# A delta-rule recurrence followed by a SoLU block: the 64x64 products of a slot in three runs, ScalarE in program order, two copies moved to it

## The chip, the core and the metric

The kernel runs on one core of a Trainium2 chip. Its engines work side by side from queues of their own: TensorE (PE; its weight loads are listed apart as PEld), VectorE (DVE), ScalarE (ACT), GpSimd (POOL) and SyncE (SP), which only issues transfers. TensorE writes to PSUM, VectorE and ScalarE read it[...]. The metric is the device time of one execution in microseconds, the median of several runs. A profiled execution gives the trace; its span runs from the first to the last instruction.

## What is computed

Two stages. The first is a recurrence over 768 time steps for 4 batches of 8 heads, with a state of 40x40 per head:

```python
y[:, :, t] = np.einsum('bhd,bhde->bhe', rt, state)
Sa = np.einsum('bhde,bhe->bhd', state, at)
state_decay = state * wt[:, :, None, :] - np.einsum('bhd,bhe->bhde', Sa, bt)
state = state_decay + np.einsum('bhd,bhe->bhde', vt, kt)
```

The result, brought to 3072 tokens of 320 numbers, goes into the second stage:

```python
h = x @ w_in                                   # 320 -> 1024
e = np.exp(h - h_max); sm = e / (np.sum(e) + 1e-09)
solu = h * sm
ln = (solu - mu) / np.sqrt(var + 1e-06) * g_ln
out = ln @ w_out                               # 1024 -> 320
```

`w_in` and `w_out` arrive as 64-bit floats, and the kernel narrows them to 32 bits itself.

## The kernel before, in words

Time is cut into chunks of 64 steps. One index i stands for one chunk of two batches (the two batches fill the 128 partitions, 64 each), so there are 24 of them; even and odd i belong to the two pairs of batches and carry separate states. Within a chunk the recurrence is written as products of 64x64 or smaller matrices, one for each of 2 batches x 8 heads, placed four at a time in the quarters of TensorE's array. A set of 16 such products is 32 instructions in the trace. The 64x64 triangular system of each head is solved through inverses of its two 32x32 diagonal blocks, computed on VectorE by elimination (`invert`, 30 steps of two operations each for two chunks at a time, L415 and L417). The blocks travel through DRAM so that they lie one per partition: `norm` stores its masked product `nt` (L388), `spread` loads the blocks (L399), `invert` stores the inverses (L422), `bring` loads them (L434, L436).

A main loop runs over slots i = -1 to 27. A slot holds work for several chunks at different stages. j = i + 5 is prepared: `decay` (logarithm of w, cumulated by a product into `pcum`, two exponentials), `decay_turned` (transposes `pei`), `scaled` (k and b times the inverse decay, on GpSimd), `front` (transposes `pa` and `pb` of a and b), `norm` (`pnt`). For i+1, `attend_kv` and `attend_rs` transpose k, v, r and the state (`pk`, `pv`, `pr`, `pst`), `scores` makes `ps`, `couple` makes `py`, `close` makes `pz`. For i, `carried` and `driven` make the right side `px` from the state and the values, `solved` applies the inverse (`pu`), `answered` makes `pl`, `read` makes the output and the new state `pyo`, `leave` takes both off PSUM. Between these stands the second stage for earlier chunks: `hidden` (products `h`, six parts of three k tiles by two halves), `exped` (maximum, exponential), `weighed` and `spreadof` (product, statistics), `folded` (transposes `plnT`), `output` (products `po`, eight of 320 columns).

In six places of a slot of the kernel before, small products stand between wide ones: `carried` and `driven`; `solved`; `norm`; `answered`; `scores` and `couple`; `close` and `read`. The part k=2 of `hidden` uses half of the array's rows. Where two groups of small products add into the same PSUM numbers from different rows of the array, `fence` (L257) drains TensorE between them: in `driven` and in the second half of `read`.

The order: TensorE, GpSimd, VectorE and SP run in the order in which the Python code calls them; only ScalarE's instructions are ordered by a scheduler. `some(n)` emits the next n elimination steps, and the tables `shares` (steps in each of four places of a slot) and `narrowed` (weights to narrow in each of two places) distribute VectorE's work. Narrowing (`split`) takes two operations on VectorE, three on ScalarE and three on VectorE for each weight tile; there are 13 of them, two before the loop and 11 in slots -1 to 3. [...]two buffers of two banks (`banks`: pu, ps, py, pnt, pl, pz, pyo, px in turn), one buffer of two banks for `h`, two buffers of one bank (`bank`: all transposes, `pcum`, `po`, `pmean`).

## Time and profile before

| | |
|---|---|
| median of 3 runs | 639.37 us (638.72 to 640.19) |
| the profiled execution | 639.79 us, its span 637.7 us |
| mean granted TensorE clock | 0.930 |
| busy: PE, DVE, POOL, ACT | 567.5, 461.9, 269.1, 245.3 us |
| weight loads (PEld) | 399.6 us |
| HBM traffic | 84 GB/s over the span |

The page of the profile gives busy time by engine, then 40 slices of the span, then queues, the chain of work that ended last, and the costliest groups. Line numbers (L254) are those of the kernel; L254 is the helper through which all small products and `h` go, so they are told apart by the tile that they write. Ends of TensorE's instructions are modelled; starts are better evidence.

### The profile page before, as it was taken

The page shows a single profiled execution, that of the slowest core. Times are in us where ns is not written, and L with a number is a line of the kernel's source. Part 1 is how long each engine was busy: PE and PEld are TensorE (multiplying, and loading weights), DVE is VectorE, ACT ScalarE, POOL GpSimd, SP SyncE. Part 2 cuts the span into 40 slices and gives each one's busy share as a digit, 9 for nine tenths or more (in the row PEclk, how much of TensorE's full clock was granted, in tenths as well). Part 3 has the DMA queues.
Part 4 walks back from the last instruction along what each step waited for, and adds up shares of the span by engine and source line. Part 5 has one row for each costly group of instructions (what it writes and reads, how often), then busy time and mean ns, then how long its engine had stood idle before and what let it go on. Part 6 is the DMA issues. An engine that isn't in the chain of part 4 may idle for free.

```text
span 637.7 us, 26729 instructions
## 1 busy us (share of the span) xinstructions
PE 567.5 (89%) x11451; PEld 399.6 (63%) x11451; DVE 461.9 (72%) x1286; ACT 245.3 (38%) x498; POOL 269.1 (42%) x444
## 2 busy tenths in 40 slices
PE   5245677988999999999999999999999999999995
PEld 3134555756577677667667767666776666766653
DVE  4678799999878778778878777787887796443431
ACT  3412545554334434433443443344243333332221
POOL 3334345574274444445543642743544642222200
PEclk9665676688999999999999999999999999999998
DMA  8939896474355535544554553654423422210000
GB/s 166 159 73 169 170 164 131 107 152 87 71 110 93 111 87 95 107 93 103 103 120 79 108 116 73 119 107 95 91 53 70 98 49 49 51 36 26 24 20 21
DMA packets 217868, 59.92 MB, mean 94 GB/s; under 512 B 203216, under 2 KB 213048, under 8 KB 217752
## 3 DMA queue, kind: packets, MB, share of 16 engines
q1 hardware_dynamic: 200984, 34.47, 31.7%
q0 software_dynamic: 11376, 19.25, 12.6%
q10 hardware_dynamic: 5392, 4.51, 2.5%
q8 instruction: 90, 1.47, 1.0%
q14 instruction: 26, 0.21, 0.1%
HBM read 40.10 MB, written 13.37 MB: 84 GB/s over the span
## 4 chain that ended last, share of the span: by engine, by line
PE 71%; DVE 13%; DMA 6%; issue 4%; ACT 2%; SPq 2%; POOL 1%; DVEq 0%; ACTq 0%; POOLq 0%
PE h L254 16%; PE po L703 14%; PE pyo L254 7%; PE px L254 4%; PE pu L254 3%; DVE uu L417 3%; PE plnT L692 3%; PE ps L254 3%; DVE prod L415 3%; PE pl L254 2%; PE pr L334 2%; PE pnt L254 2%; PE pk L334 2%; PE pa L334 2%; PE pz L254 2%
## 5 line engine op out<-in xcount | busy, mean ns | idle before, releaser
L254 PE MATMUL h<-w_in,xT 128*128 128x512 f32 (+1 forms) x288 | 121.6, 614 | 0.0
L415 DVE TENSOR_TENSOR prod<-blk,uu 128x30 f32<-128x30 f32 (+4 forms) x360 | 99.0, 275 | 24.0 <-DMA blk<-nt_dram 14.0
L703 PE MATMUL po<-w,lnT 128*128 128x320 f32 x384 | 113.5, 440 | 0.0
L417 DVE TENSOR_TENSOR uu<-uu,prod 128x30 f32<-128x30 f32 (+4 forms) x360 | 101.9, 283 | 12.4
L703 PEld LDWEIGHTS po<-w,lnT 128*128 128x128 f32 x384 | 70.5, 190 | 29.3 <-issue 2.3
L655 DVE TENSOR_REDUCE nmax<-h 128x1 f32<-128x1024 f32 x24 | 29.4, 1224 | 60.0 <-PE h L254 59.9
L388 POOL DMA_DIRECT2D nt_dram<-nt x20 | 18.3, 916 | 119.0 <-DVE nt L362 97.7
L254 PEld LDWEIGHTS h<-w_in,xT 128*128 128x128 f32 (+1 forms) x288 | 38.9, 190 | 21.9 <-issue 20.8
L623 POOL TENSOR_TENSOR st<-tot,ex 104x160 f32<-104x160 f32 x44 | 22.1, 520 | 70.4 <-DVE tot L619 68.2
L681 POOL TENSOR_TENSOR rs<-c,mhalf 128x1 f32<-128x1 f32 x24 | 13.4, 559 | 91.0 <-DVE c L680 89.6
L635 POOL DMA_DIRECT2D xT<-x x96 | 48.7, 512 | 0.0
L254 PE MATMUL pyo<-lv,kb 64*64 64x104 f32 x768 | 38.6, 274 | 6.0 <-DVE lv L362 3.3
L693 ACT COPY lnT<-plnT 128x512 f32<-128x512 f32 x48 | 26.1, 589 | 43.3 <-PE plnT L692 43.3
L399 POOL DMA_DIRECT2D blk<-nt_dram x42 | 33.3, 800 | 13.0 <-DMA nt_dram<-nt 12.7
L658 ACT ACTIVATE e<-h,nmax 128x1024 f32<-128x1024 f32 x24 | 26.8, 1115 | 28.6 <-DVE nmax L655 27.5
L254 PE MATMUL pyo<-lu,kb 64*64 64x104 f32 x768 | 37.2, 266 | 0.0
L664 DVE TENSOR_TENSOR e<-h,e 128x1024 f32<-128x1024 f32 x24 | 29.4, 1225 | 10.1 <-ACT e L658 10.1
L276 POOL DMA_DIRECT2D raw_r<-in_r_dram x48 | 34.9, 729 | 0.3 <-issue 0.3
L672 DVE BATCH_NORM_STATS2 bs<-e 128x6 f32<-128x512 f32 x48 | 30.9, 686 | 0.8
L707 ACT ACTIVATE osb<-po,rs 128x320 f32<-128x320 f32 x24 | 12.7, 528 | 48.5 <-PE po L703 29.6
L254 PEld LDWEIGHTS pnt<-aT,bT 40*64 40x64 f32 x768 | 14.6, 144 | 26.5 <-issue 25.0
L254 PEld LDWEIGHTS pyo<-lv,kb 64*64 64x64 f32 x768 | 23.9, 145 | 11.3 <-issue 7.7
(130 smaller groups left out, 1127.0 us busy)
## 6 DMA issues: line engine op xcount, KB each, us to landing
blk<-nt_dram POOLq DMA_DIRECT2D x42, 128.0 KB, 4.2
nt_dram<-nt POOLq DMA_DIRECT2D x20, 256.0 KB, 3.5
raw_w<-in_w_dram SPq DMA_DIRECT2D x48, 80.0 KB
a<-in_a_dram SPq DMA_DIRECT2D x48, 80.0 KB
raw_r<-in_r_dram POOLq DMA_DIRECT2D x48, 80.0 KB, 3.3
lv<-in_v_dram SPq DMA_DIRECT2D x48, 80.0 KB
out_dram<-osb ACTq DMA_DIRECT2D x24, 160.0 KB
raw_b<-in_b_dram SPq DMA_DIRECT2D x44, 80.0 KB
```

Of the source, the lines that this page charges most:

```text
L254: nc.tensor.matmul(o, lhsT=lhsT, rhs=rhs, start=start, stop=stop, skip_group_check=True)
L276: queue.dma_start(out=x[half(p), :, 0:D], in_=ap[2 * bp + p, :, ci * C:(ci + 1) * C, :].rearrange("h t d -> t h d"))
L334: nc.tensor.transpose(out=t[0:W2, j * P:(j + 1) * P], in_=x[:, 2 * j:2 * j + 2].rearrange("p a b -> p (a b)")[:, 0:W2], identity=ident)
L399: queue.dma_start(out=nb[home:home + Q], in_=blocks[n][:, Q * e:Q * e + Q, Q * e:Q * e + Q])
L415: nc.vector.tensor_tensor(out=t, in0=nb[:, j:j + 1, j + 1:Q].to_broadcast([P, n_c, m]), in1=u[:, 0:n_c, j:j + 1].to_broadcast([P, n_c, m]) ...
L417: nc.vector.tensor_tensor(out=u[:, 0:n_c, j + 1:Q], in0=u[:, 0:n_c, j + 1:Q], in1=t, op=ALU.subtract)
L635: nc.gpsimd.dma_start(out=xT[to:to + Q, 2], in_=x[at + P - 3 * D:at + D, 2])
L655: nc.vector.tensor_reduce(out=nmax, in_=d["h"], axis=AX.X, op=ALU.max, negate=True)
L658: nc.scalar.activation(out=e, in_=d["h"], func=AF.Exp, bias=nmax, accum_out=d["esum"])
L664: nc.vector.tensor_tensor(out=d["e"], in0=d["h"], in1=d["e"], op=ALU.mult)
L672: nc.vector.bn_stats(out=bs[:, x], in_=d["e"][:, x * 512:x * 512 + 512])
L703: nc.tensor.matmul(d["out"][:, 0:DM], lhsT=d["lnT"][:, f, :], rhs=w2[:, f, :], start=f == 0, stop=f == NF - 1)
```

## The change

The order of a slot is rewritten so that the small products stand together: `solved(i)` with `scores(i+1)`; `couple(i+1)`, `norm(j)` and `answered(i)`; `close(i+1)`, `read(i)`, `carried(i+1)` and `driven(i+1)`, the last run with the k=2 parts of `hidden` and one fence in it. The transposes of k, v and r for chunk i+2 are made at the end of slot i, the transposes of the state (`stated`) in slot i after the first run. `carried` and `driven` move one slot ahead, to the end of the slot before. ScalarE too now runs in program order. The copies of v and r into padded tiles (`by_value`) move from GpSimd to ScalarE. The logarithm (`logged`) is taken before the decays. The maximum (`highest`) is split from the exponential. `narrow` starts all its tiles before it finishes any, with two buffers of `scale`. The mean of `w_out` over its rows is copied from PSUM to SBUF before it is subtracted. Start-up loads and steps are reordered.

```diff
-        scale = two.tile([P, 512], I32, tag="scale", name="scale", bufs=1)[0:n, 0:width]
+        scale = two.tile([P, 512], I32, tag="scale", name="scale")[0:n, 0:width]
...
+    def begin_narrow(n):
         for x in range(n):
             load, part = next(parts)
-            rest = split(*part)
-            next(rest)
-            some(n_steps // n + (x < n_steps % n))
+            begun.append((load, part, split(*part)))
+            next(begun[-1][-1])
...
-            nc.gpsimd.tensor_copy(out=x.rearrange(...), in_=y.rearrange(...))
+            nc.scalar.copy(out=x.rearrange(...), in_=y.rearrange(...))
...
+    def logged(i):
+        lw = st[i]["lw"] = two.tile([P, DM], FP32, tag="lw", name="lw", bufs=1)
+        nc.scalar.activation(out=lw, in_=st[i]["raw_w"].rearrange("p h d -> p (h d)"), func=AF.Ln)
...
-                queue = nc.gpsimd if n > 1 or y and not n else nc.sync
+                queue = nc.gpsimd if n or y else nc.sync
...
-            nc.sync.dma_start(out=inverse[n][:, y::2], in_=u[C * y:C * y + C])
+            queue = nc.sync if n or not y else nc.gpsimd
+            queue.dma_start(out=inverse[n][:, y::2], in_=u[C * y:C * y + C])
...
-            nc.sync.dma_start(out=d["tu"][C * x:C * x + Q, :, Q:2 * Q], ...)
+            queue = nc.sync if i or not x else nc.gpsimd
+            queue.dma_start(out=d["tu"][C * x:C * x + Q, :, Q:2 * Q], ...)
...
     def driven(i):
-        if d["opened"]:
-            fence()
...
     def read(i, own):
-        else:
-            fence()
...
     def hidden(i, some):
-            if (kt, x) == (0, 0):
+            if (kt, x) == (NK - 1, 0):
...
-               start=kt == 0, stop=kt == NK - 1)
+               start=kt == NK - 1, stop=kt == NK - 2)
```

The start-up:

```diff
-    for n in range(3):
+    for n in range(2):
         land(n, nc.sync)
+    load_keys(2, "ba")
     decay(0)
+    logged(1)
...
         front(i)
+        front_b(i)
         decay(i + 1)
+        if i == 0:
+            logged(i + 2)
+        some(4 * (i > 1))
         norm(i)
         decay_turned(i + 1)
-        if i == 0:
-            load_keys(2, "ba")
...
             load_keys(4, "w")
+            load_values(0)
+            load_keys(1, "k")
+            load_keys(4, "ba")
+            load_keys(5, "w")
+            land(2, nc.sync)
             some(8)
...
     by_value(0)
+    begin_inverse(1)
+    attend_kv(0)
+    attend_r(0)
     scaled(2, "k")
...
+    load_keys(6, "w")
+    some(10)
+    scores(0)
     decay(5)
```

The slot, as it stands after the change (before, it runs in the order described above):

```python
        pieces = shares.get(i, (0, 5, 4, 4) if i % GRP else (3, 5, 4, 5))
        if i >= 1: bring(i + 1)
        if i >= 0: load_values(i + 2)
        narrow(0, pieces[0])

        solved(i)
        if i >= 0: scores(i + 1)
        load_keys(j + 3, "w")
        load_keys(j + 2, "bak")
        stated(i)
        front(j)
        hidden(m - 2, ((0, 1),))
        if i == 3 + LAG: centred(mean)
        narrow(some_weights[1], pieces[1])
        front_b(j)
        if ok(j + 2): logged(j + 2)
        decay_turned(j + 1)
        hidden(m - 2, ((1, 1),))
        flip(i + 1)
        highest(m - 2)
        scaled(j + 1)
        left(i - 1)
        decay(j + 2)
        output(m - 3, 0)

        some(pieces[2])
        couple(i + 1)
        exped(m - 2)
        norm(j)
        answered(i)
        weighed(m - 2)
        spreadof(m - 2)
        if ok(j) and j % GRP == GRP - 1: begin_inverse(j // GRP)
        ...
        output(m - 3, 1)

        close(i + 1)
        read(i, True)
        carried(i + 1)
        narrow(some_weights[2], pieces[3], ok(j) and j % GRP == GRP - 1)
        by_value(i + 2)
        if ok(m - 1): hidden(m - 1, ((2, 0), (2, 1)))
        fence()
        read(i, False)
        driven(i + 1)
        leave(i)
        begin_narrow(narrowed.get(i + 1, (0,))[0])
        folded(m - 2)
        hidden(m - 1, ((0, 0),))
        attend_kv(i + 2)
        hidden(m - 1, ((1, 0),))
        attend_r(i + 2)
        if i == 2 + LAG: mean = mean_ended(mean, 6)
```

Here m = i - 1. The slot before, in the same words, was: `some`, `bring`, `load_values`, `carried(i)`, `driven(i)`, `front(j)`, one part of `hidden`, loads, `narrow`; `solved(i)`, `attend_kv(i+1)`, one part of `hidden`, `norm(j)`, `attend_rs(i+1)`, the k=2 parts of `hidden`, `exped`, `decay_turned`, `scaled`, `left`; `answered(i)`, `flip(i+1)`, `weighed`, `spreadof`, `decay`, `output` first half, `begin_inverse`, `some`, `scores(i+1)`, `couple(i+1)`, `output` second half, `narrow`; `close(i+1)`, `read(i)` in both halves, `by_value(i+2)`, `leave(i)`, `folded`, two parts of `hidden`.

## The prediction

> **What bounds the kernel now.** I read the page's busy shares and slices, the chain that ended last, the engines' busy time by stretches, one slot of the timeline, and the waits of VectorE. The page first: engine, busy us (share), instructions; then tenths in 40 slices of 16 us.
>
> ```profile
> PE 567.5 (89%) x11451; PEld 399.6 (63%) x11451; DVE 461.9 (72%) x1286; ACT 245.3 (38%) x498; POOL 269.1 (42%) x444
> ...
> PE   5245677988999999999999999999999999999995
> ...
> DVE  4678799999878778778878777787887796443431
> ...
> PEclk9665676688999999999999999999999999999998
> ```
>
> Three stages: a start-up at a low TensorE clock with VectorE at nines, a long stretch in which TensorE is never idle at full clock, a short tail. The stretches say where one gives way to the other (stretch, length, then busy us of PE, PEld, DVE, ACT, POOL; clock; DMA share and GB/s):
>
> ```profile
> 92.00:114.00 22.00, 18.30 (x426) 15.04 (x422) 20.68 (x58) 10.37 (x23) 11.46 (x18) 0.66 0.68 121
> ...
> 346.00:369.00 23.00, 22.67 (x510) 15.99 (x504) 16.84 (x48) 9.23 (x19) 13.10 (x21) 1.00 0.56 109
> ```
>
> VectorE is full (20.7 of 22) until about 145 us; from 189 us TensorE is (22.7 of 23) and VectorE has 5 to 6 us to spare per slot. The chain says the same:
>
> ```profile
> PE 71%; DVE 13%; DMA 6%; issue 4%; ACT 2%; SPq 2%; POOL 1%; DVEq 0%; ACTq 0%; POOLq 0%
> ```
>
> The second products of `px` start at 188.89, 211.38, 233.86 ... 458.70: twelve intervals of 22.48 us (i=5 to 17), then 21.94, 21.37 and four of 19.79 without `front` and `norm`, up to 581.16. In this stage only the order of TensorE's instructions counts, so I took one slot's starts from the timeline (start, duration; PE rows only):
>
> ```profile
> 345.49 0.68 PE L254 MATMUL px<-st,aT 40*64 40x40 f32 x32
> ...
> 346.28 0.68 PE L254 MATMUL px<-lv,psi 64*64 64x40 f32 x32
> ...
> 346.88 0.65 PE L334 MATMUL pa<-cst,a 128*104 128x128 f32 x4
> ...
> 347.80 1.02 PE L254 MATMUL h<-w_in,xT 128*128 128x512 f32 x2
> ...
> 348.76 0.69 PE L254 MATMUL pu<-tu,x 64*64 64x64 f32 x32
> ...
> 349.27 0.63 PE L254 MATMUL pu<-x,tu 64*64 64x40 f32 x32
> ```
>
> Ends are modelled, so I use starts. A set of 32 small products inside a run takes 0.46 to 0.52 (`pu` to `pu` 0.51); the last set before wide work takes more (`px` to `pa` 0.60); the wide op before a run takes more too (`h` to `pu` 0.96, against 0.86 for the pair, which is half the chain's 1.72 for four). And `px` to `px` takes 0.79: a fence stands between.
>
> [...]the elimination op at 317.45, beside GpSimd's work, takes 0.47 where its neighbours take 0.23, and the one at 319.05, begun with GpSimd's copy of `v` (319.03), takes 0.49 against 0.2. [...]the trace's copy of `x` from PSUM has 0.43.
>
> **The change, part by part.**
>
> *Three runs instead of seven.* Entering plus leaving, from the starts in this slot (in-run set 0.49): `px` 0.10+0.11, `pu` 0.10+0.07, `pnt` 0.09+0.14, the half-row `h` 0.10+0.20, `pl` 0.14+0.13, `ps`/`py` 0.11+0.06, `pz`/`pyo` 0.22+0.12; sum 1.69. Two fences: 0.79-0.49 = 0.30 and, inside `pyo`, 0.47-0.18 = 0.29. Together 2.28. After: run 1 (`pu`, `ps`) 0.14+0.08, run 2 (`py`, `pnt`, `pl`) 0.11+0.13, run 3 (`pz`, `pyo`, `px`, half-row `h`, `pyo`, `px`) 0.34 with 0.20 for `h` inside (unseen place: 0 to 0.3), one fence 0.29 (0.2 to 0.5[...]). Sum 1.29; gain 0.99 per slot.
>
> *Waits that the new order brings.* I laid the new slot out with these durations, 0 at the first `pu`: run 1 to 2.06, `pst`, `pa`, `h`, `pb`, `pei`, `h`, `pcum` to 6.25, four `po` to 8.49, `py` 8.49, `pnt` 8.95. `pl` takes the bank pair of `py`, which ScalarE frees by `wy`: py's end + 0.14 + 0.47 = 9.6, where `pnt` ends at 9.45: a wait of 0.2 (0 to 0.4), and behind it stand `pl`, `po` and all that follows, so it counts. The bank of `pz` is wanted by `px` 1.2 us after `pz` ends; ScalarE's copy takes 0.14+0.37 behind the output's 0.53: free at +0.7, covered because it comes before the copies of `v` and `r`. Logarithm before `pei`'s copy: ready at 5.5, `pcum` at 5.6: covered by 0.1. So 0.8; adding all pieces of the new slot singly gives 21.53, a gain of 0.95. I take 0.85: a period near 21.6. Worth 14 x 0.85 = 11.9 for the intervals from i=5 to 19, and for the last four 0.76 of switches with no `pnt` and no wait for `wy`: 3.0. Together 15.
>
> *VectorE's order.* Its load per slot (17.5) fits into 21.6. In odd slots (a fresh inversion) I find `psi`, `lv`, `aT` 2.2 to 4.0, preparation 1.25, five steps, `flip` done 8.1 against `py` 8.49; maximum to 9.3, four steps, masks `nt` to 12.3 against `pz` 12.6 and `lu` to 12.9 against `pyo` 13.1; e times h to 14.05 against the next `h` bank at 14.8. All covered, by 0.2 to 0.7 us; without the cover each 1 us late costs 1 us.
>
> *Copies of `v` and `r` to ScalarE.* Two of about 0.45 (0.43 to 0.5) on an engine busy 9.2 of 22.5, between the `pz` copy and `x`: hidden by `h` and `pyo`. They wait for loads of the same slot, issued about 3 to 5 us in (`v` at 303.87), ten us before. On VectorE they take away the two held operations, 0.4 to 0.5 us per slot, which counts only in the start-up.
>
> *Start-up.* `b` and `a` of chunk 2 load before the first decay and the third weight load goes behind: the store of `nt` for chunk 1 was issued at 20.02 although its mask ended at 17.44, behind these loads on SP's queue. The chain runs through it to the blocks' landing at 30.15, so up to 2.5 us come off. Held operations: 5 x 0.4 = 2. Both halves of the first narrowing begin together: two waits of 1.6 for ScalarE become one. `mean` in SBUF: the bank is no longer kept for the 2.9 us of VectorE's subtraction at 167.4, for which `pv` waited 1.42; one ScalarE copy of 0.43 (hidden) is added; slot 4, 3.2 us over the steady period, can lose 1 to 2. Some of these cover each other: I take 6 in all (from a loss of 4, if POOL's queue, which now issues more block, store and `tu` loads ahead of `scaled`, delays `kb`, to a gain of 11). `scores(0)` and keys for chunk 0 move ahead of the loop: same instructions, nothing counted. Reversing the k order in `hidden`: the half-row parts come first, from `xT` loads that POOL issued a slot earlier; nothing.
>
> *Tail.* From 581 to 638 it is `h`, `po` and the chain maximum, exp, product; same work, one or two runs fewer in the last slot: 0.5.
>
> Sum: 15 + 6 + 0.5 = 21.5. The profiled execution took 639.79 (span 637.7 and 2.1 around it), the median is 639.37; so 639.8 - 21.5 = 618.3, say 618.
>
> **The rivals.**
>
> *A, as worked out*: 608 to 627. Chance 0.63.
>
> *B, the order eats half.* ScalarE, now in program order, and VectorE have covers of only 0.1 to 0.7. If they are late by 0.5 us per slot on average, 18 x 0.5 = 9, and the start-up gives nothing: 639.8 - 6.5 = 633. For: so many edges within 0.3. Against: before, ScalarE waits for TensorE nearly everywhere (`x` 53.1 us in total), not the reverse. Chance 0.17.
>
> *C, slower: the inversion's blocks land late.* The waits of VectorE between 210 and 480 us (waiter, releaser: us, times, longest):
>
> ```profile
> DVE nmax L655 <- PE h L254: 16.3, 12, 1.4
> DVE prod L415 <- DMA blk<-nt_dram: 9.3, 6, 1.8
> ```
>
> `norm` moves from the first third of the slot to behind `py`; its store waits for the mask near 11.5 plus 0.9 and 3.7 to landing, and the block loads on POOL's queue stand behind `rs` as well, near 16.2. Before, 8.9 us passed from the first block load (315.88) to the first product (324.75): landing 25.1, that is 3.5 into the odd slot, where the first product comes at 5.2. Cover 1.7, plus 0.3 at `flip`. Behind the waiting product on VectorE stand `flip` and the maximum, and TensorE waits for both. With nine such slots, the gain of 21.5 is gone when blocks land 2.0 + 2.4 = 4.4 us later than that; at 5 us later 9 x 3.0 = 27: 645. Against: DMA is busy only 0.45 to 0.56 of this stage. Chance 0.10.
>
> *D, the switches are not the cost*: the gaps around runs belong to the operations themselves, only the fence (0.3 x 18 = 5) and a little start-up remain, less the new wait: 636 to 640. Against: equal sets differ by 0.1 by place. Chance 0.05.
>
> *E, more*: no wait at `pl`, 1.2 per slot (21), and 11 in the start-up: 607. Chance 0.05.
>
> **How the numbers follow.** 618 is A's. The range 606 to 632 holds A, E and the better half of B: about 0.8. A difference within 0.2% is about what a measurement of this kernel cannot tell from no change: faster by over 0.2% is A, B, E and half of D with a little lost to the start-up: 0.86; within it 0.03; slower C and a bad start-up: 0.11.
>
> **What would show it.** After: period near 21.6 between `px` starts; three groups of small products per slot; `pl` waiting for `wy` by 0.2; `x` copies starting right after `px`; VectorE's `blk` waits in steady slots at most as before; i=5 reached about 6 us earlier. The prediction is wrong if TensorE shows waits for VectorE's `tu`, `lu` or `nt` of over 0.5 per slot, if `prod` waits for `blk` over 2 us, or if VectorE's full stretch at the start ends later than before.

## The result, and the profile after

The changed kernel takes 630.9 us in the median (630.28 to 633.24, 4 runs), beside 639.78 (638.72 to 640.21) for the kernel before on the same chip: a ratio of 0.987, 95% interval 0.9842 to 0.9899. A second set of six runs took 630.65 (ratio 0.985, 0.9824 to 0.9876). It is 1.3 to 1.5% faster, 9 to 10 us, where the prediction said 21.5. The profiled execution has a span of 629.0 us for 637.7. Where executions of a kernel below were over 1.5% longer than its fastest one, its time is the median of the others.

The page of the changed kernel, busy shares and slices, to be set against the same lines of before:

```profile
PE 552.8 (88%) x11451; PEld 402.9 (64%) x11451; DVE 451.9 (72%) x1286; ACT 265.6 (42%) x547; POOL 250.5 (40%) x402
...
PE   5372778698989999999999999999999999999994
...
DVE  4697877978596877869969868768698588433431
...
PEclk9666755859999999999999999999999999999998
```

The number of TensorE's instructions is the same (11451). Two copies a slot went from GpSimd to ScalarE (444 to 402 and 498 to 547 instructions), and VectorE lost 10 us of busy time. In slices 6 to 9 (some 79 to 141 us) the clock's digits are 5 5 8 5, for 7 6 6 8 before, and VectorE's row no longer stands at nines and eights in the start-up, without TensorE's being fuller. The two stretches shown of before (length, busy PE, PEld, DVE, ACT, POOL, clock, DMA share, GB/s):

```profile
92.00:114.00 22.00, 17.29 (x411) 14.89 (x410) 16.45 (x53) 11.51 (x24) 10.67 (x17) 0.60 0.66 127
346.00:369.00 23.00, 22.81 (x515) 17.04 (x508) 16.26 (x48) 10.82 (x24) 13.87 (x24) 1.00 0.64 117
```

In the steady stretch TensorE is as full as before, and gets through more in it. In the start-up VectorE falls from 20.68 to 16.45 of 22 and TensorE falls too, from 18.30 to 17.29. The chain that ended last agrees: VectorE, transfers and GpSimd have more of it than before, TensorE less (71% before):

```profile
PE 64%; DVE 15%; DMA 9%; issue 4%; POOL 3%; SPq 2%; ACT 1%; ACTq 0%; DVEq 0%; POOLq 0%
```

From one steady slot of TensorE's timeline (start, duration; the rows between are left out), the beginning of the first run and the second run:

```profile
344.25 0.69 PE L264 MATMUL pu<-tu,x 64*64 64x64 f32 x32
...
352.58 0.67 PE L264 MATMUL py<-tu,nt 64*64 64x32 f32 x32
353.07 0.67 PE L264 MATMUL pnt<-aT,bT 40*64 40x64 f32 x32
353.84 0.69 PE L264 MATMUL pl<-rT,nuT 40*64 40x64 f32 x32
```

From `pnt` to `pl` there are 0.77 us instead of 0.49: the wait for ScalarE's `wy` is there, 0.28. From `pu` to `pu` it is 21.5 to 21.7 in ten of the twelve slots from 5 to 16 (22.48 before). In VectorE's waits between 210 and 480 us, `blk<-nt_dram` and `nmax<-h`, which were at the head before, are gone; it waits for TensorE once a slot:

```profile
DVE psi L382 <- PE ps L264: 38.5, 13, 6.5
```

**Where the 8.7 us of the profiled execution come from**, by the starts of `pu`: up to slot 5 it *loses* 0.9 (191.37 to 192.26), slots 5 to 17 gain 8.3 (269.81 to 261.49), slots 17 to 23 gain 1.1 (121.64 to 120.51), the rest 0.2. So the three places in which the prediction was short are the start-up (by 6.9), the steady stretch (1.9) and the late slots (3.6). In the profiled execution of the second set the three read: 0.2 gained (slot 5 at 191.15), 9.1 gained and 1.1 gained.

The start-up's loss can be placed more closely. Slot 0 begins at 69.75 and 67.94 in these two executions, 4.2 and 6.0 earlier than before (73.91); but slots 0 to 4 then take 122.5 and 123.2 us, where they took 117.5. So the gain ahead of the loop came, and the first five slots lost it. How early slot 0 begins differs by up to 3.9 us between executions of kernels that are alike up to there (67.94 to 71.82); the lengths of slots are the better measure below.

### The profile page after: what moved, and what is told of

It reads as the page before. It is cut to its first block, busy times and chain, and to the rows that moved or that the text cites. A ratio compares the mean times of both kernels' runs of the same rounds, so it can differ in the third digit from the quotient of the medians.

```text
span 629.0 us, 26656 instructions
## 1 busy us (share of the span) xinstructions
PE 552.8 (88%) x11451; PEld 402.9 (64%) x11451; DVE 451.9 (72%) x1286; ACT 265.6 (42%) x547; POOL 250.5 (40%) x402
## 4 chain that ended last, share of the span: by engine, by line
PE 64%; DVE 15%; DMA 9%; issue 4%; POOL 3%; SPq 2%; ACT 1%; ACTq 0%; DVEq 0%; POOLq 0%
PE h L264 15%; PE po L730 14%; PE pyo L264 7%; DVE uu L437 4%; DVE prod L435 4%; PE plnT L719 3%; PE pu L264 3%; PE px L264 3%; PE ps L264 3%; PE py L264 2%; PE pz L264 2%; PE pl L264 2%; DMA w<-in_moe_w_in_dram 2%; DMA blk<-nt_dram 2%; DMA nt_dram<-nt 2%
## 5 line engine op out<-in xcount | busy, mean ns | idle before, releaser
L264 PE MATMUL h<-w_in,xT 128*128 128x512 f32 (+1 forms) x288 | 124.6, 619 | 0.0
L437 DVE TENSOR_TENSOR uu<-uu,prod 128x30 f32<-128x30 f32 (+4 forms) x360 | 97.6, 271 | 12.4
L435 DVE TENSOR_TENSOR prod<-blk,uu 128x30 f32<-128x30 f32 (+4 forms) x360 | 96.7, 269 | 11.3 <-DMA blk<-nt_dram 1.7
L382 DVE TENSOR_TENSOR psi<-ps,cst 128x512 f32<-128x512 f32 x24 | 16.6, 691 | 70.3 <-PE ps L264 70.3
L419 POOL DMA_DIRECT2D blk<-nt_dram x46 | 36.5, 800 | 26.6 <-DMA nt_dram<-nt 22.6
L264 PEld LDWEIGHTS pyo<-lv,kb 64*64 64x64 f32 x768 | 24.4, 144 | 21.7 <-issue 21.5
L476 ACT ACTIVATE wy<-py,cst 128x256 f32<-128x256 f32 x24 | 11.4, 473 | 63.2 <-PE py L264 63.2
L645 POOL TENSOR_TENSOR st<-tot,ex 104x160 f32<-104x160 f32 x44 | 21.8, 514 | 36.7 <-DVE tot L641 36.3
L561 ACT COPY x<-px 128x320 f32<-128x320 f32 x24 | 10.2, 426 | 57.9 <-PE px L264 57.9
```

Of the source, the lines that this page charges most:

```text
L264: nc.tensor.matmul(o, lhsT=lhsT, rhs=rhs, start=start, stop=stop, skip_group_check=True)
L419: queue.dma_start(out=nb[home:home + Q], in_=blocks[n][:, Q * e:Q * e + Q, Q * e:Q * e + Q])
L435: nc.vector.tensor_tensor(out=t, in0=nb[:, j:j + 1, j + 1:Q].to_broadcast([P, n_c, m]), in1=u[:, 0:n_c, j:j + 1].to_broadcast([P, n_c, m]) ...
L437: nc.vector.tensor_tensor(out=u[:, 0:n_c, j + 1:Q], in0=u[:, 0:n_c, j + 1:Q], in1=t, op=ALU.subtract)
L645: nc.gpsimd.tensor_tensor(out=to3(old), in0=to3(tot[0:W2]), in1=ex[:, :, 2 * q:2 * q + 2, C:].to_broadcast([W2, 2, 2, D]), op=ALU.mult)
```

## The experiments

"The changed kernel" below has 630.9 or 630.65 us; slot n begins with its first product `pu`.

**What one run and one fence cost.** Two kernels put back one switch each. In the first, the transposes of the state stand between `solved` and `scores`, so that a fourth run of small products begins with `ps`:

```diff
         solved(i)
+        stated(i)
         if i >= 0:
             scores(i + 1)
...
-        stated(i)
         front(j)
```

> The changed kernel with the transposes of the state between solved and scores: run 1 becomes two runs, four runs in a slot in place of three; same instructions. By the prediction's price of entering and leaving a run (0.14 to 0.34, mean 0.24) the period of a steady slot grows from 21.53 to 21.7 to 21.9 and the time by 4 to 6 us, to 635 to 637. If switches are not the cost (rival D), the period stays at 21.53 within 0.05 and the time within 1 us.

In the second, one fence more stands between `solved` and `scores`:

```diff
         solved(i)
         if i >= 0:
+            fence()
             scores(i + 1)
```

> The changed kernel with one more fence, inside run 1 between solved and scores; same instructions otherwise. By the prediction's price (0.29 to 0.30) the steady period grows from 21.53 to 21.8 and the time by 6 to 7 us, to 637 to 638. If a fence inside a run of small products costs only its own issue, the period grows by under 0.1.

Measured: 642.65 us (ratio to the kernel before 1.0039, 1.0015 to 1.0064), where 635 to 637 was forecast, and 637.38 (0.9964, 0.9948 to 0.9979), as forecast. The time is a poor measure here, since in both kernels the clock also fell to 0.50 in slot 4 (from 183 to 186 us and from 180 to 183), and slot 5 begins 5.4 and 2.2 us later than in the changed kernel. The steady period, taken where it is undisturbed, rises from 21.53 to 22.13 with the split run (21.7 to 21.9 forecast) and to 21.87 with the fence (21.8). In the chain of the changed kernel, `pu`, `ps` and `pst` take 1.07 + 0.95 + 0.58 = 2.60; with the fence 0.15 + 0.21 are added. The chain of the split kernel (start, duration):

```profile
333.28 1.19 PE ps L264 x64
...
334.50 0.69 DVE psi L382
335.19 0.60 DVE lv L382
335.79 0.61 DVE aT L373
...
336.44 0.65 PE pei L349 x4
```

`pu` and `pst` ahead of these take 1.07 and 0.57; 1.07 + 0.57 + 1.19 = 2.83: the additional run costs 0.23. The other 0.37 is a cover that is gone: `ps` ends 0.58 us nearer to `pei`, and the three masks on VectorE (1.9) no longer fit between, so TensorE waits and `pei` takes 0.65 for 0.44. A run costs 0.23 and a fence 0.34; the prediction had 1.69/7 = 0.24 and 0.30. Four runs and one fence less and the new wait for `wy` give 4 x 0.23 + 0.34 - 0.28 = 0.98, an estimate from these pieces; the undisturbed slot is 0.95 shorter. So rival D, by which the gaps are not the price of switching, is out.

**ScalarE: the order and the copies.** Five kernels take the package apart. In the new order, the copies of `v` and `r` go back to GpSimd:

```diff
-            nc.scalar.copy(out=x.rearrange(...), in_=y.rearrange(...))
+            nc.gpsimd.tensor_copy(out=x.rearrange(...), in_=y.rearrange(...))
```

> The changed kernel with the copies of v and r on GpSimd again. Prediction's step: in steady slots nothing (period 21.53 within 0.05), in the start-up VectorE loses the time of two held operations a slot, 0.4 to 0.5, so pu of slot 5 comes about 2 us later and the time is 632 to 634. If GpSimd's order is tighter than I think (its copies stand in front of the state's product), the steady period grows by 0.1 to 0.5.

It took 647.83 us (1.0107, 1.0084 to 1.013), slower than the kernel before. Not in the steady slots, of which most keep 21.5 to 21.8: slot 5 begins at 202.57, 10.3 later than in the changed kernel. The waits from 65 to 195 us (waiter, releaser: us, times, longest):

```profile
POOL bits L171 <- DVE w L195: 15.7, 3, 9.2
...
PE pv L349 <- POOL v L318: 12.3, 3, 5.6
```

GpSimd's queue holds the loads of weights, each of which waits for VectorE to have narrowed the one before; the copy of `v` stands behind them, and TensorE's transpose of `v`, now at the end of the same slot, waits for it. Then the other half of it: in the changed kernel ScalarE goes back to its scheduler (the list of engines in program order loses `Activation`).

> The changed kernel with ScalarE's instructions ordered by the scheduler again, not in program order; all other engines as changed. If ScalarE's program order is needed for the new slot (the copy of pz ahead of the copies of v and r, wy ahead of the exponential, logarithm ahead of the decays), TensorE waits for wy, for the bank of pz or for kT in every slot: period 21.8 to 22.5, time 635 to 650. If the order on ScalarE matters little, the period stays within 0.1 of 21.53 and the time within 2 us of 630.9.

It took 666.4 us (1.0407, 1.036 to 1.0453). The time hides two opposite things. Slots 5 to 17 take 304.2 us for 261.5, by the mechanism told below with the copies. But slot 5 begins at 184.77, 6.4 to 7.5 us earlier than in the changed kernel and 6.6 earlier than in the kernel before, and slots 0 to 4 take 117.2 us for the changed kernel's 122.5 and 123.2. TensorE's order, VectorE's and the transfers asked for are the same in both; only ScalarE's order differs. The end of slot 0 in the changed kernel, and then with ScalarE under its scheduler (`kT` is the copy of the transposed k, for which the next transpose waits; `scale` and `w` belong to the narrowing of weights):

```profile
92.47 0.56 ACT L184 ACTIVATE scale<-scale,top 128x320 int32<-128x320 int32 x1 [1.04 <-DVE scale L182]
93.53 0.64 ACT L191 ACTIVATE w<-w,g,g 128x320 f32<-128x320 int32 x1
94.08 0.56 ACT L358 COPY kT<-pk 104x512 f32<-104x512 f32 x1
94.69 0.65 PE L349 MATMUL pr<-cst,r 128*104 128x128 f32 x4 [1.97 <-ACT kT L358]
```

```profile
87.98 0.59 ACT L358 COPY kT<-pk 104x512 f32<-104x512 f32 x1
88.62 0.65 PE L349 MATMUL pr<-cst,r 128*104 128x128 f32 x4 [0.24 <-ACT kT L358]
89.35 0.56 ACT L184 ACTIVATE scale<-scale,top 128x320 int32<-128x320 int32 x1 [0.30 <-DVE scale L182]
```

`begin_narrow` is called ahead of `attend_kv`, so in program order three operations of the narrowing, which wait for VectorE, stand ahead of `kT`, and TensorE's transpose of r waits 1.97 us (3.04 in the second execution). The scheduler takes `kT` first. Slot 0 takes 21.63 us so, for 25.52; from 65 to 195 us the mean clock is 0.85 for 0.79. So program order on ScalarE, which saves 43 us in slots 5 to 17, costs 5 to 6 us in slots 0 to 4. One profiled execution stands beside two here. The order with `kT` ahead of the narrowing was not run, and it is not known which waits make up what slots 1 to 4 lose.

The copies alone, in the kernel before:

> The kernel before with one part of the change alone: the copies of v and r on ScalarE. With the copies back on GpSimd in the new order, the sixth slot began 10 us later, TensorE's transposes waiting 12.3 us for GpSimd's copy of v, which stood behind loads for the narrowing. Theory Q (the copies cost that only where the new order puts them, at the end of a slot behind GpSimd's queue): in the old order the move is worth my price of 2 us or nothing, 636 to 640. Rival (the move itself is worth 10 us in any order, so the rest of the new order cost the start-up 10): 628 to 631.

Both theories missed: 673.5 us (1.0536, 1.045 to 1.0621; four executions from 668.86 to 679.67, of which the longest is the profiled one). ScalarE's timeline of this kernel (start, duration, what; in brackets the idle time ahead and its releaser):

```profile
292.89 0.61 ACT L343 COPY vT<-pv 104x512 f32<-104x512 f32 x1
299.46 0.46 ACT L307 COPY v<-lv 128x320 f32<-128x320 f32 x1 [5.96 <-DMA lv<-in_v_dram]
299.82 0.58 ACT L343 COPY rT<-pr 104x512 f32<-104x512 f32 x1
```

The scheduler put the copy of `v` for two chunks on right behind `vT`; it waits 6 us for a load that was asked for in this slot, and `rT` and the state, for which TensorE waits, stand behind it. In the changed kernel under the scheduler it is the same (from 215 to 460 us ScalarE waits 36.1 us for `lv`, in ten slots, and `pcum` 24.3 for ScalarE's `bT`). Last, the kernel before with ScalarE in program order, without and with the copies:

> The kernel before with one edit: ScalarE in program order; nothing moved. Theory P (program order is needed only because of the copies, which the scheduler puts ahead of a transpose's copy; the old order of calls serves ScalarE too): 636 to 644. Rival (the old order of calls is poor for ScalarE, the scheduler mended it): 650 to 680.

> The kernel before with two edits together: ScalarE in program order, and the copies of v and r on it. With the copies alone under the scheduler, ScalarE waited 6 us for a load with the copy of v put ahead of the turned r and the state, and the time was 679. Theory P: in program order the copy stands behind the other work of the slot, so against the run with the order alone the two held VectorE operations a slot come off in the start-up, 0 to 4 us less. Rival (the load comes late for ScalarE wherever the copy stands): 10 us or more above the run with the order alone.

685.57 us (1.0714, 1.0698 to 1.073) and 685.48 (1.0715, 1.0698 to 1.0731). So the first went the rival's way and beyond its range (650 to 680). The copies by themselves, in this order, are worth 0.1 us, which is nothing within the intervals of some 1 us: neither the 2 us of the prediction nor a loss. What program order costs the old order of calls is in its chain (start, duration):

```profile
306.98 1.23 DVE nmax L655
...
309.25 0.19 ACT e L658
309.45 0.48 ACT ex L350
309.92 0.38 ACT lw L315
...
310.35 0.81 PE pcum L317 x2
```

`exped` is called ahead of `decay_turned` and `decay`, so in program order `ex` and the logarithm stand behind the exponential, which waits for the maximum. TensorE's `pcum` waits 20.1 us for the logarithm from 215 to 460 us; the rest of the 46 us was not followed. The change calls the logarithm and the maximum earlier. By this chain these edits, to which the prediction gave a cover of 0.1 us and no price, help to make program order possible; no run leaves them out of the changed kernel alone. Program order in turn makes the copies on ScalarE possible. None of the parts that were tried alone was a gain, and leaving one out of the changed kernel cost some 17 us (copies on GpSimd) or 35 (ScalarE under its scheduler).

**The mean of w_out.** It is read from PSUM again, in slot 4:

```diff
-                                    in1=mean.unsqueeze(1).to_broadcast([P, NF // 2, DM]), op=ALU.subtract)
+                                    in1=mean[:, 0:DM].unsqueeze(1).to_broadcast([P, NF // 2, DM]), op=ALU.subtract)
...
         if i == 3 + LAG:
-            centred(mean)
+            centred(mean_ended(mean, 6))
```

> The changed kernel with the mean of w_out subtracted from PSUM as before: its second half is computed in slot 4, and no copy is kept in SBUF. Prediction's step: the change gained 1 to 2 us in slot 4, so slot 4 (24.5 in the changed kernel, pu to pu) grows to 25.5 to 26.5 and the time to 632 to 633. If other waits hide it, slot 4 stays within 0.5.

632.18 us (0.9871, 0.9853 to 0.9889), no difference from the changed kernel (0.987 and 0.985), though with a slot 4 of 27.58 for 24.50. But slot 4 also took 27.57 in the kernel with one fence more, in which the mean is in SBUF. A stretch of slot 4 behind the wait (columns as above), first of the changed kernel, then of the one with the fence:

```profile
180.00:183.00 3.00, 3.00 (x40) 1.99 (x40) 2.72 (x10) 1.04 (x2) 0.00 (x0) 1.00 0.03 5
```

```profile
180.00:183.00 3.00, 3.00 (x44) 2.29 (x37) 2.76 (x10) 0.88 (x2) 0.05 (x1) 0.50 0.03 5
```

In both TensorE waits 2.6 us here for the turned inverse `tu`. In one the granted clock stays at 1.00, in the other it falls to 0.50 for some 7 us, and the slot is 3 us longer. It fell there also with the split run (0.50 from 183 to 186 us) and with the mean in PSUM (0.56 from 180 to 183 us). With unread products in TensorE's waits (next part), where `pz` of slot 4 takes 0.67 us as in a steady slot, the mean was tried again:

> The mean of w_out read from PSUM in slot 4 as before the change, with the unread products in the start-up. With the mean in PSUM and no such products slot 4 took 27.6 us for 24.5, but in two other runs with the mean in SBUF slot 4 also took 27.5, and in all of these the granted clock fell to 0.50 there. Theory K (clock): with the clock held up the mean is worth under 2 us: 628 to 630. Rival (the mean itself is worth the 3 us of slot 4): 631 to 632.

627.93 us (0.9827, 0.9788 to 0.9866), the same as with the mean in SBUF (627.93; slots 3 and 4 together 49.8 us, 49.6 in SBUF). The mean is worth nothing that was measured; the 3 us go with the fall of the clock (1.00 in the slot of 24.50, 0.50 and 0.56 in those of 27.57 and 27.58).

**The start-up: transfers and VectorE's order.** Three kernels. The load of chunk 7's `w` ahead of the weights' loads, since `pcum` of slot 0 waited 6.0 us for it:

```diff
     load_keys(5, "bak")
+    load_keys(7, "w")
     for n in (3, 4, len(lands)):
...
-        load_keys(j + 3, "w")
+        if i >= 0:
+            load_keys(j + 3, "w")
```

> The changed kernel with one load moved: w of chunk 7 is loaded ahead of the three weight loads at the end of the start-up, not behind them. In the changed kernel the product pcum of slot 0 waits 5.99 us for the logarithm of this load, and comes at 81.5 us, as in the kernel before, though all ahead of it is 4 us earlier. Theory T (a transfer swallowed the start-up's gain): pcum of slot 0 comes 4 to 5 us earlier, pu of slot 5 comes 3 to 5 us earlier than 192.3, the time is 626 to 628 against 630.9. Theory O (in the start-up slots VectorE and TensorE wait for each other by their order, mostly flip behind elimination steps): pcum comes earlier, but other waits take its place by slot 2, pu of slot 5 stays within 1.5 us, the time is 629.5 to 632.

631.64 us (0.9865, 0.9839 to 0.9892). The wait fell to 3.7, others took its place (`py` for `tu` 13.2 for 11.6), and slot 5 began at 192.79: no gain. The opposite, 1 MB more to move:

> The changed kernel with one more transfer between the steps ahead of the loop and the loop, on ScalarE's queue: 1 MB of w_in copied from DRAM to DRAM, which nothing reads. In ten kernels so far the second slot began between 93.6 and 96.1 us although the first began anywhere between 68.1 and 74.0, and the DMA share from 70 to 95 us was 0.86 to 0.96. Theory D (transfers set the end of the first slot, so that a head start ahead of the loop is lost there): at the 180 GB/s of that stretch 1 MB takes 5.8 us, so the second slot begins 3 to 6 us later, at 98 to 101, and the time is 634 to 637. Rival (VectorE and the weights' narrowing set it; transfers have room): 95 to 96, and 630 to 632.

629.8 us (0.988, 0.9841 to 0.9919). This does not decide between the two. First, ScalarE's queue came to the added transfer at 47.9 us, well ahead of slot 0, and it was moved by 55 us, so the stretch from 70 to 95 us that the theory speaks of had no more to move (DMA share 0.88, and 0.87 without). The stretch in which it was moved, in the changed kernel and then with the addition (columns as above):

```profile
45.00:50.00 5.00, 2.39 (x70) 1.71 (x66) 4.52 (x18) 1.65 (x4) 2.90 (x4) 1.00 0.52 103
```

```profile
45.00:50.00 5.00, 3.27 (x76) 2.29 (x74) 4.43 (x18) 2.38 (x6) 2.60 (x4) 1.00 0.98 246
```

Second, the profiled execution (slots 0 and 1 2.3 and 2.1 us later, slot 5 at 192.38, where it began without) is one of four at 629.2 to 629.8; the other three took 634.6 to 636.6 and left no trace. What speaks against transfers is the kernel with ScalarE under its scheduler: with the same transfers its slot 5 begins 6.4 to 7.5 us earlier. Then the turning of the inverse (`flip`) ahead of narrowing and elimination steps, in slots 0 to 4 and 18 to 23:

```diff
+        early = i in EARLY
+        if early:
+            flip(i + 1)
         narrow(some_weights[1], pieces[1])
...
-        flip(i + 1)
+        if not early:
+            flip(i + 1)
         highest(m - 2)
```

> The changed kernel with flip(i+1) ahead of the second place of elimination steps and narrowing, in slots 0 to 4 and 18 to 23 only. In the changed kernel py waits for flip 11.6 us in all in slots -1 to 4, and 2.7 us in slots 19 and 20. Theory O: the waits of py in slots 1 to 4 fall from 6.8 to under 2 us, pu of slot 5 comes 4 to 7 us earlier, slots 19 and 20 together 2 to 3 us shorter, the time is 622 to 626. Theory T: the waits move to other places (loads, low TensorE clock), pu of slot 5 within 1.5 us, only the late slots gain: 627.5 to 630.

639.72 us (0.9991, 0.9972 to 1.001): the whole gain lost. `py` waits less for `tu` (5.0 us), but `pz` now waits for `nt` (9.4, for 1.4 in the changed kernel), and slot 19 took 28.0, because `flip` there waited with all of VectorE behind it for the store of the inverse (4.5 us) and its load (4.8).

**The start-up: the clock.** TensorE's two largest waits from 55 to 192 us, of the kernel before and then of the changed one:

```profile
PE pyo L254 <- DVE lv L362: 7.4, 4, 3.1
PE pr L334 <- ACT kT L343: 4.5, 3, 1.9
```

```profile
PE py L264 <- DVE tu L464: 11.6, 5, 4.9
PE pcum L332 <- ACT lw L323: 8.3, 3, 6.0
```

The wait for `tu` was 1.9, once, before. The wait for `tu` alone is not what ScalarE's order costs: under its scheduler, where slot 5 begins at 184.77, `py` waits 13.5 us for `tu`. What comes behind such waits can be seen in slot 2 (TensorE's timeline of the changed kernel):

```profile
124.42 1.44 PE L332 MATMUL pcum<-lw,cst 128*128 128x320 f32 x2 [2.16 <-ACT lw L323]
126.12 1.08 PE L264 MATMUL py<-tu,nt 64*64 64x32 f32 x32 [0.27 <-DVE tu L464]
...
134.26 2.08 PE L264 MATMUL h<-w_in,xT 64*128 64x512 f32 x4
```

Steps are nearly twice as long as in the steady slot (`py` 1.08 for 0.67, the half-row `h` 2.08 for 1.13): the clock is 0.50 from 123 to 140 us. Waits of 1.39 us ahead of `pei` and 2.16 ahead of `pcum` go ahead of the fall, with TensorE busy 0.88 of 3 us from 120 to 123. What TensorE did while it stayed there is told below. So unread products (320 columns, operands that lie in SBUF) were put where TensorE waits in slots 0 to 4 (21 of them):

```diff
+            t = bank("pwarm")
+            for _ in range(n):
+                nc.tensor.matmul(t[:, 0:320], lhsT=ident, rhs=cst[:, 0:320], start=True, stop=True)
...
+        warm(i, "pei")
         decay_turned(j + 1)
...
+        warm(i, "pcum")
         decay(j + 2)
...
+        warm(i, "py")
         couple(i + 1)
```

> The changed kernel with added products whose results nothing reads (ident times 320 columns of the constants), put on TensorE in slots 0 to 4 where it waits for VectorE or ScalarE: 6 ahead of pcum in slot 0, 3 ahead of py in slot 1, 2 ahead of pei and 3 ahead of pcum in slot 2, 3 and 4 ahead of py in slots 3 and 4. In the changed kernel TensorE idles 4 of 8 us from 120 to 129 us, and its granted clock is 0.50 from 123 to 139 us, through pz, pyo, px, h. Theory K (the low clock of the start-up lost what was expected): though TensorE gets more work, its clock in slots 2 to 4 is mostly 1.0, slot 2 (pu to pu) falls from 27.4 to 22 to 24, pu of slot 5 comes 3 to 6 us earlier, the time is 625 to 628. Theory O (VectorE's order and load set the start-up whatever the clock): slot 2 may shorten, but pu of slot 5 comes within 1.5 us of 192.3, the time is 629.5 to 633.

627.93 us (0.981, 0.9787 to 0.9833), some 3 us faster with more work. Slot 2 takes 25.90 us for 27.40 (22 to 24 forecast), and slots 0 to 4 take 120.9 for 122.5 and 123.2; so the clock is worth about 2 us here. The rest comes later and is another matter (last part). As a control, 17 such products in slots 0 to 2 of the kernel before:

> The kernel before with unread products of 320 columns on TensorE in slots 0 to 2, ahead of the transposes of r and ahead of the output's products, where it waited for VectorE or ScalarE (17 in all); such products made the changed kernel 3 us faster. Theory K1 (the low clock is part of the shortfall: the kernel before alternates less and loses little by it): 638.5 to 641. Rival K2 (both kernels lose as much by the clock in the start-up, so that it explains nothing of the difference): 636 to 637.5.

643.3 us (1.0041, 1.0024 to 1.0058): slower by 2.8, beyond the range of either theory, on the side of the first. From 65 to 195 us the mean granted clock was 0.83 before and 0.79 after; with the products it was 0.87 and 0.88. So a higher clock won time in the changed kernel and not in the kernel before, where the products stood at other places; whether better places would have paid there was not tried.

**The start-up: slot 4.** To the unread products is added that in slot 4 five elimination steps stand ahead of the mask, where VectorE was idle, and two instead of six ahead of `flip`:

```diff
-    shares = {..., 4: (0, 6, 5, 6)}
+    shares = {..., 4: (5, 2, 4, 6)}
```

> The changed kernel with the unread products of the run before last, and in slot 4 five elimination steps ahead of the first product's mask, where VectorE sat idle, and two instead of six behind it (5, 2, 4, 6 for 0, 6, 5, 6). Theory V (in slot 4 the product py waited 2.6 us for the turned inverse, which stood behind the subtraction of the mean and six steps): slot 4 shrinks from 24.5 to about 22 us and the time from 627.9 to 625.5. Rival (VectorE's sum over the slot sets its length wherever the steps stand): 627 to 629.

626.74 us (0.9805, 0.9784 to 0.9826), less than forecast: TensorE waited no more for `tu` in slot 4, but four of the unread products stood in its place, and the slot took 23.86 us for 24.49. Without these four:

> The run with five steps moved in slot 4, without the four unread products ahead of py in slot 4. In that run TensorE waited for nothing in slot 4, and yet the slot took 23.9 us, 21.5 and some 1.8 for these four products and 0.5 else. Theory: they are now on the path of a full TensorE, slot 4 takes about 22 us and the time is 625. Rival (without them the clock falls in slot 4): 627 to 630.

624.26 us (0.9737, 0.9714 to 0.976), as forecast, and the fastest version here: 2.6% below the kernel before, and 1% below the changed one, which took 630.65 on the same chip. Slot 4 takes 21.75, slots 0 to 4 take 117.4, as much as before the change (117.5), and from 160 to 215 us TensorE has one wait, of 0.7 for `lnT`. The transpose of r still waits for `kT`, 6.1 us in two slots.

> The changed kernel itself once more, for a narrower interval beside the others of this chip: 629 to 633.

That is the second set named at the beginning (630.65).

**The late slots.** Slot 19 took 21.8 us for 19.8 before. Its chain in the changed kernel:

```profile
494.43 6.02 DMA blk<-nt_dram
...
504.65 0.45 DVE tu L464
...
505.24 0.67 PE py L264 x32
```

The blocks landed late, `flip` stood behind five steps, and `py` waited 1.2 us. Steps were spread otherwise in slots 17 and 19:

```diff
-    shares = {..., 4: (5, 2, 4, 6)}
+    shares = {..., 4: (5, 2, 4, 6), 17: (0, 5, 5, 6), 19: (0, 0, 8, 5)}
```

> As the run with five steps moved in slot 4, and in slots 17 to 19 the steps spread so that the inversion used in slot 19 ends earlier and no step stands ahead of the turned inverse in slot 19 (slot 17: 0, 5, 5, 6 for 0, 5, 4, 4; slot 19: 0, 0, 8, 5). Theory L (the late slots lost 2 us because slot 19's first elimination step waited for its blocks, with the turned inverse behind it): slot 19 shrinks from 21.8 to about 19.8 us and the time by 2 against the run without it. Rival (the turned inverse is late because its own load is): no difference.

630.4 us (0.9861, 0.9843 to 0.988), 3.7 more than without, so neither theory held. `flip` came at 497.75, as wished, but the eight steps now stood ahead of `lu`; `pyo` waited for it, the clock fell behind the wait to 0.50 (`pyo` 2.52 us for 1.21, `h` 2.01 for 1.06), and slot 19 took 26.4.

**Stalls that no edit aimed at.** In the changed kernel TensorE's timeline has four stalls with no releaser, all inside `ps` (in brackets the idle time ahead). The two longest:

```profile
412.30 0.34 PE L264 MATMUL ps<-rT,vT 40*64 40x64 f32 x6 [1.27 <-issue]
...
499.06 0.57 PE L264 MATMUL ps<-rT,vT 40*64 40x64 f32 x23 [1.40 <-issue]
```

With 0.60 at 194.9 and 0.33 at 539.5 they are 3.6 us together. They stand at the same instructions, 5, 6, 23 and 6 ahead of the end of `ps`, in the second execution of the changed kernel (0.34, 0.99, 1.12, 0.32) and in the kernel with `w` loaded first. With 1 MB more to move the third is missing (slot 19 then took 20.2 us for 21.8) and the others are there. In the kernels with unread products ahead of them, that is with more instructions on TensorE's queue, none of the four is there; others of 0.2 to 1.3 us turn up elsewhere, in the fastest version one of 0.84 in slot 11. The kernel before has none. This points to a place in the queue of instructions. Each of the four came in the second half of 128 small products in a row. The DMA share of the one or two microseconds ahead was 0.46 to 1.16, but it was as high where no stall came (1.25 from 321 to 323 us, 0.69 in the two microseconds behind). Slots 5 to 23 take 378.25 us in the fastest version and 382.0 in the changed kernel: 3.6 - 0.84 = 2.8 of these 3.75 are stalls. That TensorE's instructions themselves come late is what this suggests; no run was made that shows it, and it stays open.

## Why the prediction was right or wrong, point by point

- **Three runs instead of seven**: right. Forecast 0.24 per run and 0.30 per fence, measured 0.23 and 0.34. The steady period is 21.53 in undisturbed slots: the direct sum of the pieces said 21.53, and the 0.85 taken for it was 0.1 too careful.
- **Waits that the new order brings**: right. `pl` waits 0.28 for `wy` (0.2, range 0 to 0.4); `px` does not wait for the bank of `pz`.
- **14 x 0.85 = 11.9**: of the twelve slots from 5 to 16 six gave 0.95 and four 0.8, but the other two lost 1.9 in stalls inside `ps`, which no row of the kernel before showed. Twelve times 0.85 is 10.2, measured are 8.3 and, in the second set, 9.1.
- **The last four slots, 3.0, and slots 17 to 19, 1.7**: mis-sized. Together 1.1 instead of 4.7. Slot 19 lost 1.4 in a stall and 1.2 by the mechanism of rival C (blocks late, `flip` behind the steps); without the stall it took 20.2. In the steady slots C did not occur: VectorE never waits for `blk` there. The rest of the 3.6 is not explained.
- **VectorE's order, "all covered, by 0.2 to 0.7 us"**: right in the steady slots (beside the stalls TensorE has one wait there, of 0.4 us). It was read for a full TensorE, and the same order was not costed for the start-up, where the covers are not there.
- **Copies of `v` and `r`**: hidden on ScalarE in the steady slots, as said (0.46 us each). The 2 us for VectorE's operations beside GpSimd's work in the start-up failed: measured 0.1, in the old order. Two such operations of one slot (0.47 and 0.49 us) are all that the trace of before was shown to have; what lengthens them was not shown, so the 2 us were the author's estimate. And the step missed that the copy had to leave GpSimd's queue: some 17 us otherwise.
- **ScalarE in program order and the logarithm, in the steady slots**: treated as covers. They are conditions; in the old order of calls program order costs 46 us.
- **The mean in SBUF, 1 to 2 us**: failed, nothing.
- **Start-up, "I take 6 in all"**: this is the step that failed, and half of the shortfall. The gains ahead of the loop that it adds up did come: slot 0 began 4.2 to 6.0 us earlier, and VectorE's busy time from 65 to 195 us fell from 115.3 to 103.0. What the sum left out is ScalarE's program order. The prediction looked at it only in a steady slot, where it is covered (the logarithm by 0.1 us), and put it at nothing in the start-up, where ScalarE also narrows weights and waits for VectorE while it does. Measured: slots 0 to 4 take 122.5 and 123.2 us in program order, 117.2 with ScalarE under its scheduler, 117.5 in the kernel before. So the order costs 5 to 6 us there and takes back what had been won; with the scheduler slot 5 begins 6.6 us earlier than before the change, near the 6 of the prediction, but then each slot behind pays more. The clock was also lower (0.79 from 65 to 195 us, and 0.83 before the change): with unread products in the waits it was 0.88, and about 2 us were won, and the steps of slot 4 spread otherwise won 2.7 more in that slot. Which of ScalarE's operations costs what is shown for slot 0 alone.
- **The rivals**: B, the order eats half, came nearest in time (633). It named ScalarE's program order and a start-up that gives nothing, and that is what came; its loss of 0.5 us in every slot is not there, the steady slots are whole. So B's number fits in part by luck. D is refuted by the split run.
- **"What would show it"**: of the signs of an error that the prediction named, TensorE's wait for `tu` in the start-up was the one that came.

## What to carry to other kernels

Cost a new order of work twice: where the bounding engine is full, and where it waits, since there a saving on one engine may be only a longer wait of another (here 12 us less of VectorE's busy time, and slots 0 to 4 longer by 5 to 6), and behind TensorE's waits its clock may be low (here 0.50 for 17 us behind waits of 1.39 and 2.16 us). An order on one engine's queue can be right for one stage and wrong for another: compare an undone part stage by stage, since a total that is 35 us worse hid a start-up that was 5 to 6 us better. Parts of a change that look free (a program order, an earlier call, a copy on another engine) can be conditions of one another; undo them one at a time before giving any of them a price. And a gain measured after adding or removing instructions may be the place of a stall: look for it in the timeline before crediting the edit.

## What the runs showed of the hardware that was not expected

- The granted clock stayed at 0.50 for 17 us (123 to 140) in slot 2 of the changed kernel, although TensorE was busy 2.84, 1.86, 3.00 and 2.91 of 3 us in the stretches from 126 to 138. These were for the most part small products; whether that is the reason no run shows. With two and three wide unread products in the waits ahead, it was back at 1.00 from 126 us on, and `py`, at 127.88, took 0.67 us for 1.08.
- After the same wait of 2.6 us in slot 4 the clock fell to 0.50 with one more fence and stayed at 1.00 in the changed kernel; the slot with the fall is 3 us longer (27.57 for 24.50).
- Stalls of 0.3 to 1.4 us inside 128 small products in a row repeat at the same instruction from run to run, and are elsewhere when instructions are added ahead of them.
